# First pair's keys hashed in two halves, and the last output block transposed on TensorE

## Chip, cores and metric

The kernel runs on 1 core of one Trainium2 chip. The metric is device time in microseconds (us) for one execution: the median of three runs. The kernel before takes 908.99 us (runs: 909.02, 906.41 and 908.99). A separate profiled execution took 907.58 us, of which the profile's span is 905.8 us; all positions in time below are counted from the start of that span.

TensorE, the matrix engine, is PE in the profile, and its weight loads are PEld; VectorE is DVE, ScalarE is ACT, GpSimd is POOL and SyncE is SP. A "q" after an engine's name (SPq, ACTq) is its instruction queue, where it issues DMAs.

## What is computed

There are two parts. First an attention in which a query sees only the keys of its own hash bucket; the bucket is made of the signs of six random projections. Its output, turned into a matrix of 3072 tokens by 512, then goes through a feed-forward layer with a squared ReLU.

```python
# q, k, v: (4 batches, 8 heads, 768 positions, 64), proj: (64, 6)
q_bits = (einsum('bhsd,dk->bhsk', q, proj) > 0)
k_bits = (einsum('bhsd,dk->bhsk', k, proj) > 0)
mask   = bucket(q_bits)[..., :, None] == bucket(k_bits)[..., None, :]
scores = where(mask, q @ k.T / 8, -1e9)
attn   = softmax(scores)
x      = (attn @ v) arranged as (3072, 512)
h      = x @ w_in                    # (3072, 2048)
out    = (max(h, 0) ** 2) @ w_out    # (3072, 512)
```

## The kernel before: the parts that are touched

The attention works on 16 pairs of heads, one head on partitions 0 to 63 and the other on 64 to 127. For each pair it needs transposed queries and keys (`feat`) and their hash bits as numbers (`bits`): a score is the product of the bits of key and query, which is hugely negative if any bit differs, plus the product of their features. For all pairs but the first, `features` and `prepare` make these beside the scores of the pair before. The first pair has nothing to hide behind, so this is the head of the kernel.

```python
with tc.manual_schedule():              # every engine works in program order
    load_first()                        # q, k of pair 0: head 0 on SP's queue, head 1 on ACT's
    nc.vector.memset(busy, 1.0)
    keep_busy(8)                        # matmuls on dummy data
    make_identity(nc, ident)
    constants()                         # loads proj, see below
    load_pair(1); load_values(0)
    for i in range(2): load_weight(i)
    first_features(0, 0)                # 3 TensorE transposes of q, copied out by ACT
    first_features(0, 1)
    keep_busy(2, 256)
    first_features(1, 0)                # 3 TensorE transposes of k (keys 0 to 383), copied by DVE
    hash_bits(0, turn("hash"), (0,))    # projections of q: 4 matmuls, PSUM
    first_features(1, 1)                # keys 384 to 767
    banks = turn("hash")
    for c in range(2):
        hash_bits(0, banks, (1,), (c,)) # projections of k: 2 matmuls for each half
    keep_busy(4)
    signs(0, 0)                         # 4 ACT activations: the bits of q
    first_keys()                        # DVE: the bits of k
    for pr in range(NP):
        ...
        score(pr, 0)                    # keys 0 to 127
        score(pr, 1)
        ...                             # score(pr, 2) to (pr, 5); keys 384 on from (pr, 3)

def constants():
    nc.gpsimd.memset(projs, 0.0)
    for h in range(2):
        nc.gpsimd.dma_start(out=projs[h * D:(h + 1) * D, 0:N], in_=proj)
    ...

def first_keys():
    bits[0, 1] = t = all_bits[0][1]
    for c in range(2):                  # c: half of the keys
        ...
        for h in range(2):
            nc.vector.tensor_scalar(out=t[...], in0=hashed[0, 1][...], scalar1=0.0, op0=ALU.is_gt)
        nc.vector.tensor_scalar(out=t[:, cut], in0=t[:, cut], scalar1=spans, scalar2=bases, ...)

def turn(name):                         # a PSUM tile of two banks; 3 take turns
    return ps_s.tile([P, 2, 512], FP32, name=name, tag="turn")
```

The feed-forward layer multiplies by a scheme of Strassen's kind in two levels. One `product` makes seven small products; in the last one of the kernel, `use(m, ...)` is `fourth(m, ...)`, which adds up a block of 128 output columns by 256 tokens and closes it. The output comes out transposed (columns on partitions). `put_out` turns it in blocks of 32 by 32 on DVE and writes it with four DMAs, whose runs in DRAM are 32 values long.

```python
def product(n, w, at, bt, c11, c12, c21, c22, hook=None):
    ...
    c11(acc[1], one)                    # fourth(0)
    add(0, at(4), ...); two = keep(0, "two")
    add(2, at(3), ...); five = keep(2, "five")
    add(0, at(5), ...); three = keep(0, "three")
    add(2, at(6), ..., last=True)
    c12(acc[2], two)                    # fourth(1): closes columns 0 to 127, both halves
    c22(three, five)                    # fourth(3)
    add(0, at(2), bt["t4"], last=True)  # the last 8 matmul passes of the kernel
    c21(acc[0])                         # fourth(2): the last block

def fourth(n, one, two):
    add_to(out_block(1, 0, n), block(W, n), whole(one, two))
    close(1, 0, n)

def close(ih, jh, n):                   # columns 128 to 255 of the last block: each half by itself
    ...
    if (i, ih, jh, n // 2) == (NCHUNK - 1, 1, 0, 1):
        lo = n % 2 * QN
        put_out(i, ih, jh, n // 2, o[0][:, lo:lo + QN], lo)
    elif o[1] == 2:
        put_out(i, ih, jh, n // 2, o[0])

def put_out(i, ih, jh, n, o, lo=0):
    ot = p_y.tile([P, HN], FP32, name="ot", bufs=2)[:, 0:w]      # two buffers in turn
    nc.vector.transpose(out=ot, in_=o)
    for a in range(P // 32):
        queue = nc.gpsimd if (ih, jh) == (1, 1) else nc.sync
        if (i, ih, jh) == (NCHUNK - 1, 1, 0) and a % 2:
            queue = nc.scalar
        queue.dma_start(out=out[at, ...].rearrange("(c i) j -> i c j", i=32), in_=ot[...])
```

After that every engine reads a flag (`slow`) and jumps over a general version of the kernel, which these inputs don't need. SP waits for all outstanding DMAs, and the program ends.

Of the kernel before, what the change touches and what calls it, by code (L numbers as in the profile page):

```python
# [34 lines left out]
def kernel(  # L35
# [10 lines left out]
    nc = tc.nc  # L46
# [174 lines left out]
    def constants():  # L221
        N = NBITS
        nc.gpsimd.memset(projs, 0.0)
        for h in range(2):
            nc.gpsimd.dma_start(out=projs[h * D:(h + 1) * D, 0:N], in_=proj)
# [126 lines left out]
    def first_keys():  # L352

        bits[0, 1] = t = all_bits[0][1]
        for c in range(2):
            at = slice((2 + c) * NR_B, (3 + c) * NR_B)
            cut = slice(c * HS, (c + 1) * HS)
            for h in range(2):
                nc.vector.tensor_scalar(
                    out=t[h * D:h * D + NR_B, cut], in0=hashed[0, 1][at, h, 0:HS],  # L360
                    scalar1=0.0, scalar2=None, op0=ALU.is_gt,
                )
            nc.vector.tensor_scalar(
                out=t[:, cut], in0=t[:, cut], scalar1=spans, scalar2=bases, op0=ALU.mult,
                op1=ALU.add,
            )

# [188 lines left out]
    with tc.manual_schedule():  # L556
        load_first()
        nc.vector.memset(busy, 1.0)
# [11 lines left out]
        hash_bits(0, turn("hash"), (0,))  # L570
        first_features(1, 1)
        banks = turn("hash")
        for c in range(2):
            hash_bits(0, banks, (1,), (c,))
        keep_busy(4)
        signs(0, 0)
        first_keys()
# [3 lines left out]
        for pr in range(NP):  # L581
# [20 lines left out]
            score(pr, 0)  # L602
            score(pr, 1)
# [221 lines left out]
        def put_out(i, ih, jh, n, o, lo=0):  # L825


            w = o.shape[1]
            ot = p_y.tile([P, HN], FP32, name="ot", bufs=2)[:, 0:w]
            nc.vector.transpose(out=ot, in_=o)  # L830
            m0 = ih * HD + n * P
            at = slice(i * NCH + jh * HN + lo, i * NCH + jh * HN + lo + w)
            for a in range(P // 32):
                queue = nc.gpsimd if (ih, jh) == (1, 1) else nc.sync
                if (i, ih, jh) == (NCHUNK - 1, 1, 0) and a % 2:
                    queue = nc.scalar
# [3 lines left out]
                )  # L840

        def project(i):
# [12 lines left out]
            def close(ih, jh, n):  # L855
                o = outs[ih, jh, n // 2]
                o[1] += 1
                if (i, ih, jh, n // 2) == (NCHUNK - 1, 1, 0, 1):

                    lo = n % 2 * QN  # L860
                    put_out(i, ih, jh, n // 2, o[0][:, lo:lo + QN], lo)
                elif o[1] == 2:
                    put_out(i, ih, jh, n // 2, o[0])
# [357 lines left out]
```

## Time and profile before

| Engine | Busy, us | Share of the span | Instructions |
|---|---|---|---|
| PE | 884.4 | 98% | 4372 |
| PEld | 504.5 | 56% | 4372 |
| DVE | 697.6 | 77% | 1012 |
| ACT | 363.4 | 40% | 593 |
| POOL | 91.4 | 10% | 149 |

The granted TensorE clock is 0.996 of full speed over the span. The chain that ended last spends 93% of its time on PE and 3% on DMA. Read the page for the middle of the kernel, where PE is always busy; for its two ends, the totals hide everything, and the timeline and the chain have to be asked for the first 20 us and the last 20 us alone.

### The profile page before, as it was taken

The page shows a single profiled execution, that of the slowest core. Times are in us where ns is not written, and L with a number is a line of the kernel's source. Part 1 is how long each engine was busy: PE and PEld are TensorE (multiplying, and loading weights), DVE is VectorE, ACT ScalarE, POOL GpSimd, SP SyncE. Part 2 cuts the span into 40 slices and gives each one's busy share as a digit, 9 for nine tenths or more (in the row PEclk, how much of TensorE's full clock was granted, in tenths as well). Part 3 has the DMA queues.
Part 4 walks back from the last instruction along what each step waited for, and adds up shares of the span by engine and source line. Part 5 has one row for each costly group of instructions (what it writes and reads, how often), then busy time and mean ns, then how long its engine had stood idle before and what let it go on. Part 6 is the DMA issues. An engine that isn't in the chain of part 4 may idle for free.

```text
span 905.8 us, 11897 instructions
## 1 busy us (share of the span) xinstructions
PE 884.4 (98%) x4372; PEld 504.5 (56%) x4372; DVE 697.6 (77%) x1012; ACT 363.4 (40%) x593; POOL 91.4 (10%) x149
## 2 busy tenths in 40 slices
PE   8999999999999999999999999999999999999994
PEld 3444444444444444443688854445888644458884
DVE  5788899798998885887777776677778666777874
ACT  5878878887788761222211112221111122221110
POOL 2000000000000000564000011112000211100002
PEclk9999999999999999999999999999999999999998
DMA  9577769778977326999765735557757455545575
GB/s 180 107 146 139 198 175 204 172 251 210 233 182 162 112 99 185 279 273 287 253 219 159 178 67 151 152 151 221 278 150 183 75 151 152 149 130 159 144 188 82
DMA packets 253407, 158.14 MB, mean 175 GB/s; under 512 B 166496, under 2 KB 215648, under 8 KB 253344
## 3 DMA queue, kind: packets, MB, share of 16 engines
q1 hardware_dynamic: 218448, 84.04, 39.4%
q10 hardware_dynamic: 24160, 37.89, 14.4%
q0 software_dynamic: 10736, 35.40, 12.8%
q8 instruction: 36, 0.59, 0.3%
q14 instruction: 27, 0.22, 0.1%
HBM read 119.28 MB, written 38.01 MB: 174 GB/s over the span
## 4 chain that ended last, share of the span: by engine, by line
PE 93%; DMA 3%; DVE 2%; ACT 1%; issue 1%; ACTq 0%; DVEq 0%
PE acc L675 57%; PE st L385 17%; PE xo L412 14%; PE tot L430 3%; PE hash L337 2%; DMA w_unit<-w_in 2%; DMA k_nat<-in_k_dram 1%; ACT bits L347 1%; ACT e L389 0%; DVE peaks L716 0%; DVE b L765 0%; DMA out_dram<-ot 0%; DMA leaf<-w_out 0%; DVE h L764 0%; DVE t L491 0%
## 5 line engine op out<-in xcount | busy, mean ns | idle before, releaser
L389 ACT ACTIVATE e<-st 128x1024 f32<-128x1024 f32 x192 | 145.2, 810 | 67.7 <-PE st L385 62.7
L675 PE MATMUL acc<-x,w_unit 128*128 128x512 f32 x384 | 169.6, 593 | 1.8 <-DMA w_unit<-w_in 1.8
L385 PE MATMUL st<-feat,feat 64*128 64x512 f32 (+1 forms) x768 | 150.4, 483 | 0.0
L412 PE MATMUL xo<-e,v_nat 128*64 128x512 f32 (+1 forms) x768 | 134.8, 492 | 0.0
L675 PE MATMUL acc<-b,leaf 128*128 128x256 f32 x600 | 133.0, 379 | 0.0
L675 PE MATMUL acc<-t_x,w_unit 128*128 128x512 f32 x288 | 127.8, 593 | 0.0
L675 PEld LDWEIGHTS acc<-x,w_unit 128*128 128x128 f32 x384 | 72.8, 190 | 92.7 <-issue 89.2
L675 PEld LDWEIGHTS acc<-b,leaf 128*128 128x128 f32 x600 | 113.8, 190 | 17.1 <-issue 1.7
L412 PEld LDWEIGHTS xo<-e,v_nat 128*64 128x64 f32 x768 | 51.4, 136 | 82.4 <-issue 70.3
L675 PEld LDWEIGHTS acc<-t_x,w_unit 128*128 128x128 f32 x288 | 54.5, 190 | 69.8 <-issue 67.7
L385 PEld LDWEIGHTS st<-feat,feat 64*128 64x128 f32 x768 | 66.1, 188 | 34.9 <-issue 26.8
L402 DVE TENSOR_TENSOR total<-total,e 128x1536 f32<-128x1536 f32 x48 | 84.2, 1753 | 1.7
L764 DVE TENSOR_TENSOR h<-acc,two 128x512 f32<-128x512 f32 x24 | 16.6, 691 | 86.2 <-PE acc L675 86.2
L675 PE MATMUL acc<-t,leaf 128*128 128x256 f32 x336 | 76.6, 380 | 0.8 <-ACT one L682 0.4
L682 ACT COPY two<-acc 128x512 f32<-128x512 f32 (+1 forms) x45 | 21.9, 486 | 131.8 <-PE acc L675 113.3
L347 ACT ACTIVATE bits<-hash,lifts 32x384 bf16<-32x384 f32 x124 | 70.9, 572 | 7.1 <-issue 3.5
L675 PEld LDWEIGHTS acc<-t,leaf 128*128 128x128 f32 x336 | 63.6, 190 | 10.5 <-DVE t L491 1.1
L682 ACT COPY one<-acc 128x512 f32<-128x512 f32 (+1 forms) x45 | 21.9, 486 | 117.0 <-PE acc L675 75.2
L765 DVE SCALAR_TENSOR_TENSOR b<-h 128x512 f32<-128x512 f32 x96 | 64.2, 690 | 2.5
L385 PE MATMUL st<-bits,bits 64*128 64x256 bf16 (+1 forms) x384 | 63.2, 325 | 2.4 <-ACT e L389 1.2
L675 PE MATMUL acc<-b_t,leaf 128*128 128x256 f32 x240 | 54.2, 380 | 1.3 <-issue 1.3
L675 PEld LDWEIGHTS acc<-b_t,leaf 128*128 128x128 f32 x240 | 45.4, 190 | 8.1 <-issue 2.0
(125 smaller groups left out, 871.4 us busy)
## 6 DMA issues: line engine op xcount, KB each, us to landing
leaf<-w_out ACTq DMA_DIRECT2D x142, 256.0 KB, 3.0
w_unit<-w_in SPq DMA_DIRECT2D x24, 896.0 KB, 6.0
raw<-in_moe_w_in_dram SPq DMA_DIRECT2D x16, 512.0 KB, 5.5
raw<-in_moe_w_out_dram SPq DMA_DIRECT2D x16, 512.0 KB, 4.7
w_out<-sums POOLq DMA_DIRECT2D x16, 448.0 KB, 7.0
v_nat<-in_v_dram SPq DMA_DIRECT2D x16, 384.0 KB, 4.9
x_all<-x_t SPq DMA_DIRECT2D x16, 384.0 KB, 3.1
x<-x_all POOLq DMA_DIRECT2D x3, 2048.0 KB, 13.0
```

The source lines that it names most:

```text
L337: nc.tensor.matmul(out=banks[g * NR_B:(g + 1) * NR_B, h, 0:HS], lhsT=projs[rows], rhs=feat[pr, w][rows, c * HS:(c + 1) * HS], start=True, ...
L347: nc.scalar.activation(out=t[h * D:h * D + NR_B, c * HS:(c + 1) * HS], in_=hashed[pr, w][at, h, 0:HS], func=ACTF.Sign, scale=HUGE, bias=li ...
L385: nc.tensor.matmul(out=st[:, h, 0:hi - lo], lhsT=src[pr, 1][rows, key], rhs=src[pr, 0][rows, lo:hi], start=first, stop=not first,)
L389: nc.scalar.activation(out=e[:, :, lo:hi], in_=st[:, :, 0:hi - lo], func=ACTF.Exp, scale=scale)
L402: nc.vector.tensor_tensor(out=totals[pr], in0=in0, in1=weights[pr, kt][:, :, 0:S], op=ALU.add)
L412: nc.tensor.matmul(out=xo[h * D:(h + 1) * D, lo:hi], lhsT=nat[pr, "v_nat"][:, h, kt * D:(kt + 1) * D], rhs=weights[pr, kt][:, h, lo:hi], s ...
L430: nc.tensor.matmul(out=tot[g * 32:(g + 1) * 32, 0:HS], lhsT=ones, rhs=src[:, h, c * HS:(c + 1) * HS], start=src is totals[pr], stop=src is ...
L675: nc.tensor.matmul(out=acc[to], lhsT=a(i), rhs=b(i), start=first and i == 0, stop=last and i == n - 1, skip_group_check=True,)
L682: nc.scalar.copy(out=t, in_=acc[of])
L764: nc.vector.tensor_tensor(out=h, in0=one, in1=two, op=ALU.add)
L765: nc.vector.scalar_tensor_tensor(out=out[:, r], in0=h, scalar=0.0, in1=h, op0=ALU.max, op1=ALU.mult)
```

## The change

At the head of the kernel it makes two changes. The projections (`proj`) are loaded from ACT's queue, behind the keys, instead of from GpSimd's. The keys of the first pair are hashed and weighed in two halves: keys 0 to 383 at once, before the second half of the keys is even transposed, and keys 384 to 767 only after the first score tile, since the scores need them only from `score(0, 3)` on. The purpose is to let the first scores start earlier.

At the end, the last 128 output columns of the last block (two halves of 256 tokens) are no longer turned in 32 by 32 blocks on DVE. Two TensorE transposes each turn them whole into PSUM, ACT copies one half out and DVE the other, and each half is written with one DMA, whose runs in DRAM are 128 values long. Of the four DMAs of the block before, the two that went over ACT's queue go over GpSimd's. The purpose is to shorten the chain behind the last matmul.

```diff
     def constants():
-        nc.gpsimd.memset(projs, 0.0)
-        for h in range(2):
-            nc.gpsimd.dma_start(out=projs[h * D:(h + 1) * D, 0:N], in_=proj)
...
-    def first_keys():
-        bits[0, 1] = t = all_bits[0][1]
-        for c in range(2):
...
+    def first_keys(c, banks):
+        if c == 0:
+            bits[0, 1] = all_bits[0][1]
+        t = bits[0, 1]
+        hash_bits(0, banks, (1,), (c,))
+        at = slice((2 + c) * NR_B, (3 + c) * NR_B)
+        cut = slice(c * HS, (c + 1) * HS)
+        for h in range(2):
             nc.vector.tensor_scalar(
+                out=t[h * D:h * D + NR_B, cut], in0=banks[at, h, 0:HS],
+                scalar1=0.0, scalar2=None, op0=ALU.is_gt,
             )
+        nc.vector.tensor_scalar(
+            out=t[:, cut], in0=t[:, cut], scalar1=spans, scalar2=bases, op0=ALU.mult, op1=ALU.add,
+        )
...
     with tc.manual_schedule():
+        nc.vector.memset(busy, 1.0)
+        nc.vector.memset(projs, 0.0)
         load_first()
-        nc.vector.memset(busy, 1.0)
+        for h in range(2):
+            nc.scalar.dma_start(out=projs[h * D:(h + 1) * D, 0:NBITS], in_=proj)
...
         hash_bits(0, turn("hash"), (0,))
+        signs(0, 0)
+        first_keys(0, turn("hash"))
         first_features(1, 1)
-        banks = turn("hash")
-        for c in range(2):
-            hash_bits(0, banks, (1,), (c,))
         keep_busy(4)
-        signs(0, 0)
-        first_keys()
...
             score(pr, 0)
+            if pr == 0:
+                first_keys(1, turn("hash"))
             score(pr, 1)
...
                 if (i, ih, jh) == (NCHUNK - 1, 1, 0) and a % 2:
-                    queue = nc.scalar
+                    queue = nc.gpsimd
...
+        def put_last(n, o):
+            row, col = n // 2, n % 2
+            tp = ps_m.tile([P, 512], FP32, name=f"acc{col}")[:, 0:QN]
+            for t in range(QN // P):
+                nc.tensor.transpose(out=tp[:, t * P:(t + 1) * P], in_=o[...], identity=ident)
+            ot = p_y.tile([P, HN], FP32, name="ot", bufs=2)[:, 0:QN]
+            if col:
+                nc.scalar.copy(out=ot, in_=tp)
+            else:
+                nc.vector.tensor_copy(out=ot, in_=tp)
+            lo = (NCHUNK - 1) * NCH + col * QN
+            (nc.sync if col else nc.scalar).dma_start(
+                out=out[lo:lo + QN, HD + row * P:HD + (row + 1) * P].rearrange(
+                    "(t p) j -> p t j", p=P),
+                in_=ot.rearrange("p (t j) -> p t j", j=P),
+            )
...
                 if (i, ih, jh, n // 2) == (NCHUNK - 1, 1, 0, 1):
-                    lo = n % 2 * QN
-                    put_out(i, ih, jh, n // 2, o[0][:, lo:lo + QN], lo)
+                    put_last(n, o[0][:, n % 2 * QN:(n % 2 + 1) * QN])
```

## The prediction

> **What bounds the kernel now.** I read the page first: PE is busy 98% of 905.8 us, so only what lengthens or shortens PE's own line counts, and PE's line has slack only at its two ends. The change touches nothing between. So I asked the chain of waits for the first 20 us.
>
> ```profile
> 1.28 5.19 DMA k_nat<-in_k_dram
> ...
> 6.51 0.55 PE tp L300 x3
> 7.06 1.35 PE hash L337 x8
> 8.41 0.48 PE tp L300 x3
> 8.89 1.49 PE hash L337 x8
> 10.37 0.97 PE xo L317 x4
> 11.34 0.80 issue
> 12.14 6.12 PE st L385 x42
> ```
>
> The columns are start, length, what. Until 6.5 us the first keys are on their way. Then everything is one line: transpose keys, hash queries, transpose the other keys, hash both halves, dummy matmuls, and at 12.14 us the first score. Two views say what holds these steps: the waits of the first 32 us (first line below), and VectorE's timeline.
>
> ```profile
> PEld hash L337 <- DMA projs<-in_proj_dram: 0.4, 1, 0.4
> ```
>
> ```profile
> 10.50 1.12 DVE L359 TENSOR_SCALAR bits<-hash 32x384 bf16<-32x384 f32 x2 [1.02 <-PE hash L337]
> 11.66 0.38 DVE L363 TENSOR_SCALAR bits<-bits,spans,bases 128x384 bf16<-128x384 bf16 x1
> 12.07 1.13 DVE L359 TENSOR_SCALAR bits<-hash 32x384 bf16<-32x384 f32 x2
> ```
>
> The projections come 0.4 us late. And DVE begins the bits of keys 0 to 383 only at 10.50, when both halves are hashed; they are done at 12.04, and the scores start. So the first score waits for DVE, and DVE waits for a hash of keys that no one needs yet.
>
> For the other end, DVE's timeline from 892 us on:
>
> ```profile
> 893.48 0.71 DVE L830 STREAM_TRANSPOSE ot<-o 128x512 f32<-128x512 f32 x1
> 894.12 0.38 DVE L815 TENSOR_TENSOR tmp<-three,five 128x256 f32<-128x256 f32 x1
> 894.54 0.43 DVE L815 TENSOR_TENSOR o<-sum,tmp 128x256 f32<-128x256 f32 x1
> 896.03 0.45 DVE L830 STREAM_TRANSPOSE ot<-o 128x256 f32<-128x256 f32 x1 [1.07 <-DMA out_dram<-ot]
> 896.40 0.38 DVE L815 TENSOR_TENSOR o<-sum,acc 128x256 f32<-128x256 f32 x1
> 897.64 0.45 DVE L830 STREAM_TRANSPOSE ot<-o 128x256 f32<-128x256 f32 x1 [0.85 <-DMA out_dram<-ot]
> ```
>
> PE's last matmul ends at 894.19. DVE then waits twice for a free `ot` buffer, and its last transpose ends at 898.09, with nothing computed in between that takes long. The issues behind it are worse (SyncE's queue, the timeline cut at 896 us; ScalarE's shows the same at 896.92):
>
> ```profile
> 896.86 2.23 SPq L837 DMA_DIRECT2D out_dram<-ot  x1
> ```
>
> The others of its kind take 0.3 to 0.6 us. The last two DMAs of either queue go out at 899.19 and 899.65 and land by 902.03. Meanwhile SP jumps over the general version; the waits of its queue have `SPq L1051 <- SPq L1051: 2.7`, from 900.86 to 903.57. Then some twenty semaphore checks and the last barrier take 2.2 us to 905.8.
>
> **What the Trainium skill says.** "VectorE: DVE Perf Modes", section "The three transpose paths": DVE transposes in 32 by 32 blocks, TensorE turns a full 128 by 128 but into PSUM, which a copy must empty. The trace agrees on the cost: three fp32 transposes take 0.55 us, 384 columns out of PSUM 0.48 us on ACT and 0.56 us on DVE. "DMA: Bandwidth & Descriptors", section "Anatomy of one DMA — SWDGE (gpsimd) path": a fixed cost of about 2 us, nearly all of it completion. Here output DMAs at the end take 2.1 to 4.3 us to landing, median 2.8, so fewer DMAs behind each other save issues, not that floor. "Runtime: NRT & Kernel Launch", section "Instruction fetch mechanics": engines stream instructions in 16 KiB blocks, and a jump out of the window waits for a fetch. SP's 2.7 us at its jump fits; ACT's took only 0.4 us, so it is not certain to recur. I take the 2.2 us stall for such a fetch too: a 16384-byte packet of the instruction queue starts at 896.9 and takes 1.8 us. That is a guess.
>
> **Head, step by step.** (a) The projections' 64 small packets go behind the keys on ACT's queue. The last packet of those keys starts at about 5.6 us and the keys land at 6.47, so I put the projections at 6.6 to 6.9 instead of 7.52. The queries' hash (from 6.99) then runs through: from 7.57 its six remaining passes took 0.84 us, and all eight together, on separate parts of the array, should take the same, so it ends at 7.83, not 8.41. (b) The keys' first half, two matmuls: the same two took 0.83 us (8.82 to 9.65). They end near 8.6. (c) DVE: 1.12 + 0.38 us and gaps, as before 1.54 us from its start to its end: from 8.7 to 10.25. (d) ACT's four activations for the queries' bits: 2.35 us, now from 7.95, done at 10.3. Both inputs are there by 10.3, and the dummy matmuls (transposes 8.6 to 9.1, then 1.0 us) are through at 10.1. First score at 10.35: 1.8 us earlier. (e) The second half's hash now stands between two score tiles; two fp32 matmuls of 384 columns with two passes each keep PE 0.7 us (second half's start less the first's, 9.54 - 8.82). Net: 1.8 - 0.7 = 1.1 us. ACT doesn't take it back: its exponentials are about 1.6 us for a key tile, like PE's 1.62. The second half's bits, on DVE, come at about 14.5, and `score(0, 3)` needs them after 15.9.
>
> All that follows moves 1.1 us forward as one piece: pair 1's loads land at about 13, DVE takes them at 18.27; the first weights land at about 17 to 18, DVE needs them at 20.02.
>
> **End, step by step,** on the old clock. c22 comes before the last eight matmuls in program order, so PE's two transposes for that block now stand before them, and they wait for DVE's sum, ready at 894.97. PE, which would have gone on at 892.5, stands still until 895.05. Then 2 transposes 0.4 us, with the eight passes (0.217 us apart) overlapping: last matmul out at 897.2, 3 us later than before. DVE's sum 0.4 us: 897.65. Transposes 0.45: 898.15. DVE's copy of 256 columns, 0.4: 898.6. One DMA on ACT's queue, 0.45 to issue and 2.3 from its start to landing: 901.0. The `ot` buffer is free in time: GpSimd issues its two DMAs (0.65 us each) by 895.5, landed by about 898.1. The ACT half goes out at about 896.5. The old clock had 902.03 for the last landing and 903.57 for SP past its jump; SP now issues its last DMA near 896.9 instead of 900.20 and has jumped by 900.3 at the latest. So the closing checks start at 901.0 instead of 903.57, and I expect a saving of 2.6, of which I keep 2.2 for stragglers. Sum: 1.1 + 2.2 = 3.3 us.
>
> **The rivals.** First: the new wait of PE takes everything back. PE idles 2.5 us behind DVE; if transposes or semaphores cost 0.3 us more at each of four hand-overs, or if GpSimd's final drain (6.1 us before, from 892.27 to 898.37) runs 6.1 us from 895.6, to 901.7, or ACT's jump takes SP's 2.7 us (to 902.4), the end is worth only 1 to 1.5 us; total about 906. For it speaks that all three closing paths lie within 1.5 us of each other. Second: ACT's two extra issues, 0.5 us each, delay its table load (1.28 us, from 1.98) to about 3, ending at 4.3; its first copy is at 5.53, so this is hidden. But if the projections' packets queue until 7.5, (a) is void and the head gives 0.6 us: total 906. Third: a slot of the three PSUM tiles is lost to the second hash, and `score(0, 2)` waits for DVE's compare behind it; the head then gives 0.5 us. Against it: the compare ends 1.2 us after the hash, and PE works over 1.6 us on `score(0, 1)` meanwhile. Fourth: the saving is eaten in the middle. PE waits once there, 1.8 us for `w_unit<-w_in` at 419 us, a DMA of 13.7 us; its issue is set by PE's own progress, so it should move along, but its length can change by a microsecond either way.
>
> **Range and chances.** The three runs before spread over 2.6 us, the profiled one is 907.58, and the mean of all four is 908.0; a median of three is uncertain by about 1 us. 908.3, between that and the median, less 3.3 is 905.0. Adding spread of the runs, the rivals' 1 to 2 us and a possible fetch stall or its absence (2 us), eight in ten lie in 902.4 to 907.8. 2% is 18 us; the head lasts 12 us and the end 12, so neither can reach it: same 0.98.
>
> **What would show it.** Right: the first score near 10.4 us, no wait for `projs`, `hash` matmuls after the first score tile, PE idle about 2.5 us near the end in front of its transposes, last landing about 2 us after DVE's last copy. Wrong: a `projs` wait at the first hash, the first score later than 11.2, PE waiting for ACT at the third score tile, a closing chain through GpSimd's drain or through ACT's jump, or a changed wait in the middle.

## The result and the profile after

The changed kernel takes 906.82 us (median of six runs, 905.91 to 909.7) and the kernel before, on the same chip, 908.04 us (six runs, 906.41 to 909.02). The ratio is 0.9994, with a 95% interval of 0.9975 to 1.0013: no difference that can be measured; the interval leaves room for a saving of some 2.3 us at most. The prediction was 905.0 us, with eight chances in ten for 902.4 to 907.8. The total is inside. The saving of 3.3 us that it was worked out from is not.

The two profiled spans are 905.8 us before and 904.1 us after, so the profile seems to show 1.7 us of the 3.3. To see where they lie I cut every span into three pieces at two points of the trace that all kernels here share: the start of the second pair's scores, which closes the head, and the start of VectorE's sum `o` for columns 0 to 127 of the last block, where the code of the end begins.

| Span, us | Head | Middle | End | All |
|---|---|---|---|---|
| before | 31.69 | 861.33 | 12.78 | 905.8 |
| after | 31.76 | 859.58 | 12.74 | 904.1 |

Neither end got shorter. The 1.7 us lie in the middle, which the change doesn't touch. So each end has to be asked what it gained and what it gave back.

**Head.** The chain that ended last in the first 20 us of after; columns are start, length and what:

```profile
1.99 5.64 DMA projs<-in_proj_dram
...
7.76 1.18 PE hash L334 x12
8.95 0.56 ACT bits L344
...
10.71 0.58 ACT bits L344
11.34 1.77 PE st L384 x11
13.11 0.77 PE hash L334 x4
13.88 4.44 PE st L384 x30
```

Before, this chain ran through the keys and TensorE. Now it begins with the projections, which are on their way for 5.64 us and land at 7.63 (and 7.94 for the second). The first hash starts at 7.76, not at 6.99. Then ScalarE's four activations, the queries' bits, take up to 11.29, and the scores wait for them. The first score tile of one head starts at 10.74, the other's at 11.34; before it was 12.14 us. At 13.11 the moved hash takes 0.77 us out of the row of scores. VectorE, which the prediction had ready at the same time as ScalarE, was done with the first half's bits at 10.58:

```profile
9.05 1.12 DVE L358 TENSOR_SCALAR bits<-hash 32x384 bf16<-32x384 f32 x2 [1.02 <-PE hash L334]
10.20 0.38 DVE L362 TENSOR_SCALAR bits<-bits,spans,bases 128x384 bf16<-128x384 bf16 x1
```

**End.** TensorE's timeline of after from 889 us on; the bracket holds the idle time ahead of a group and what ended it:

```profile
889.75 1.03 PE L676 MATMUL acc<-b_t,leaf 128*128 128x256 f32 x4
893.33 0.62 PE L847 MATMUL acc<-ident,o 128*128 128x128 f32 x2 [2.56 <-DVE o L816]
893.75 3.43 PE L676 MATMUL acc<-b_t,leaf 128*128 128x256 f32 x8
897.69 0.44 PE L847 MATMUL acc<-ident,o 128*128 128x128 f32 x2 [0.52 <-DVE o L816]
```

TensorE stands still for 2.56 us in front of the transposes, as predicted. But the eight passes behind them then take 3.43 us, 0.427 us apart, where the prediction had 0.217. The table of stretches says why (the columns: stretch, its length, busy time of PE, PEld, DVE, ACT and POOL with their instructions, granted TensorE clock, DMA share, GB/s):

```profile
894.00:896.00 2.00, 2.00 (x6) 1.55 (x6) 0.00 (x0) 0.36 (x1) 0.10 (x1) 0.50 0.78 138
```

The clock has fallen to half, from 893.45 to 896.86. VectorE's last two operations, and the first waits of SP's queue in that stretch:

```profile
897.22 0.42 DVE L816 TENSOR_TENSOR o<-sum,acc 128x256 f32<-128x256 f32 x1 [3.94 <-PE acc L676]
898.17 0.42 DVE L854 COPY ot<-acc 128x256 f32<-128x256 f32 x1 [0.53 <-PE acc L847]
```

```profile
SPq L1070 <- SPq L1070: 6.5, 2, 3.5
```

The last copy ends at 898.6 and its DMA goes out at 898.62. The 6.5 us of SP are two things that the line doesn't keep apart. From 895.46 to 898.40 it is its jump over the general version. The other 3.5 us, by the semaphore records, are a wait for one DMA, the last: 15 of its 16 parts have landed by 900.47, the sixteenth lands at 902.15, SP goes on at 902.17, and the rest of its closing list takes the 1.9 us to the end.

### The profile page after: what moved, and what is told of

Read it like the earlier page. It is cut to its first block, busy times and chain, and to the rows that moved or that the text cites. A ratio compares the mean times of both kernels' runs of the same rounds, so it can differ in the third digit from the quotient of the medians.

```text
span 904.1 us, 11898 instructions
## 1 busy us (share of the span) xinstructions
PE 886.7 (98%) x4376; PEld 506.3 (56%) x4376; DVE 697.6 (77%) x1012; ACT 364.2 (40%) x594; POOL 91.7 (10%) x148
## 4 chain that ended last, share of the span: by engine, by line
PE 91%; DMA 4%; DVE 2%; ACT 1%; issue 1%; POOL 0%; ACTq 0%; DVEq 0%
PE acc L676 55%; PE st L384 17%; PE xo L411 14%; DMA w_unit<-w_in 3%; PE tot L429 3%; PE hash L334 2%; ACT bits L344 1%; DMA projs<-in_proj_dram 1%; DVE peaks L717 0%; DMA out_dram<-ot 0%; DVE b L766 0%; ACT e L388 0%; DVE ot L830 0%; DVE h L765 0%; DVE o L816 0%
## 6 DMA issues: line engine op xcount, KB each, us to landing
x<-x_all POOLq DMA_DIRECT2D x3, 2048.0 KB, 13.1
```

## The experiments

All were cut at the same two points. "First score" is where a score matmul first starts; "last out" is the end of the last pass of the kernel's products, counted from the start of the end piece; "landing" is when the last part of the last output DMA has landed, counted likewise. "Time" is the run's own measured time, single except where said.

| Run | First score | Head | Middle | Last out | Landing | End | Time |
|---|---|---|---|---|---|---|---|
| before | 12.14 | 31.69 | 861.33 | +1.16 | +9.01 | 12.78 | 908.04 (median) |
| before_again | 12.20 | 31.76 | 860.63 | +1.16 | +8.95 | 12.53 | 906.69 |
| h_only | 10.94 | 31.95 | 861.09 | +1.16 | +9.08 | 11.89 | 906.71 |
| t_only | 12.37 | 31.93 | 861.26 | +5.62 | +10.61 | 12.68 | 907.71 |
| after | 10.74 | 31.76 | 859.58 | +5.84 | +10.81 | 12.74 | 906.82 (median) |
| h_early | 10.83 | 31.60 | 861.08 | +5.42 | +10.31 | 12.38 | 906.83 |
| t_warm | 10.91 | 31.93 | 864.19 | +4.16 | +9.15 | 11.08 | 909.01 |
| t_defer | 10.78 | 31.81 | 861.93 | +1.16 | +10.62 | 12.55 | 908.05 |
| t_defer_own | 11.06 | 32.08 | 860.36 | +1.16 | +7.31 | 10.20 | 904.41 |
| h_noins | 13.23 | 32.80 | 861.57 | +4.16 | +8.38 | 10.31 | 906.44 |
| h_noins2 | 10.74 | 30.87 | 860.27 | +5.03 | +9.44 | 11.36 | 904.27 |
| h_sp | 11.22 | 32.23 | 860.49 | +4.16 | +8.83 | 10.76 | 905.26 |
| t_best | 10.81 | 31.82 | 860.71 | +1.16 | +7.66 | 10.52 | 904.82 |
| best | 10.86 | 30.99 | 861.34 | +1.16 | +7.67 | 9.45 | 903.75 (median) |

The kernel before, measured beside the single runs, gave single times between 906.9 and 911.6 us, and the middle alone differs by 2.3 us (859.58 to 861.93) among kernels that share its code (t_warm aside). So single times decide nothing here; the pieces do.

### The change taken apart: before_again, h_only, t_only

My theory was that the head gains at its first score and gives it back, that the end loses what it gains to the clock, and that the middle is scatter. The rival was that the middle's 1.7 us is an effect of the earlier head. `before_again` is the kernel before without an edit, `h_only` is after with before's end, `t_only` is after with before's head.

```diff
 # h_only, against after
-                    queue = nc.gpsimd
+                    queue = nc.scalar
-                    put_last(n, o[0][:, n % 2 * QN:(n % 2 + 1) * QN])
+                    lo = n % 2 * QN
+                    put_out(i, ih, jh, n // 2, o[0][:, lo:lo + QN], lo)
 # t_only, against after (before's load of proj on GpSimd and before's order again)
-        signs(0, 0)
-        first_keys(0, turn("hash"))
         first_features(1, 1)
+        banks = turn("hash")
+        for c in range(2):
+            hash_bits(0, banks, (1,), (c,))
         keep_busy(4)
+        signs(0, 0)
+        first_keys()
```

> The kernel before, once more, for the scatter of its three stretches: head (start of pair 1's scores, 31.76 us in the chain of the first profile), middle (from there to the start of VectorE's sum o for columns 0 to 127 of the last block, 893.02) and tail (from there to the end of the span, 12.78). Theory 'middle is scatter': head within 0.2 us, tail within 0.5 us, middle off by up to 2 us, mostly at the wait for w_unit at 419 us. Rival 'the change moved the middle': middle within 0.3 us of the first profile, 1.7 us longer than after's.

> The changed head alone, with the end of before. Theory 'late projections and an inserted hash': pair 1's scores start at 31.8, as in after (31.83) and before (31.76); the first hash waits for projs until about 7.6 again, and the second hash takes 0.7 to 0.8 us between the first two key tiles. Rival 'the head lost its gain by chance in that one profile': they start at 30.7. Tail as before: 12.8 us.

> The changed end alone, with the head of before. Theory 'clock and stragglers': PE stands still some 2 us in front of its transposes, its clock drops, the last eight passes are 0.43 us apart instead of 0.22, and the tail is 12.8 us as in before and after; if the clock's drop happens to fall after the passes, it is 11 to 11.5. Rival 'the tail's changes need the changed head': none expected. Head 31.76.

Measured: the head piece is 31.69 and 31.76 us in the two profiles of before, 31.93 in `t_only` (before's head), and 31.76 and 31.95 in after and `h_only` (the new head). The new head has its first score 1.2 to 1.4 us earlier than the first profile of before, and arrives at the second pair at the same time or later. The middle is 860.63 in `before_again`, 0.7 shorter than in the other profile of the same kernel, and 861.09 in `h_only`. So the rival does not hold: with the new head alone, the middle is no shorter than in `before_again`. `t_only` has the end of after, 12.68 us, with the head of before: what happens at the end belongs to the end. Its clock fell too, from 894.78 to 898.20.

`h_only` also shows that before's end is not always 12.78: here it is 11.89. The long DMA issue on SP, which the prediction counted in, is not in it.

What the middle's scatter is made of can be seen at one place. The waits of TensorE from 415 to 470 us, first in before and then in after (us in total, times, longest):

```profile
PE acc L675 <- DMA w_unit<-w_in: 1.8, 1, 1.8
```

```profile
PE acc L676 <- DMA w_unit<-w_in: 1.1, 1, 1.1
```

The weights that TensorE waits for there were 13.73 us on their way before and 13.02 us after. That is 0.7 of the 1.7 us. Laid side by side instruction by instruction, TensorE's records show after gaining at four more places, 0.5 us at 222 us and 0.2 each at 461, 532 and 649. `before_again`, which has no edit, gains 0.4 at the first of them and 0.2 at the last. No run shows that the change had a hand in any of them.

### The head: who holds the first score

After `h_only` there were two questions. Do the projections come late because they stand behind the keys on ScalarE's queue, or because nothing small gets through while the first loads run? And does the moved hash cost what the earlier start gains? `h_early` issues the projections ahead of everything, on GpSimd's queue; `h_sp` ahead of the queries, on SP's.

```diff
 # h_early, against after (memset of projs moved to GpSimd as well)
-        load_first()
         for h in range(2):
-            nc.scalar.dma_start(out=projs[h * D:(h + 1) * D, 0:NBITS], in_=proj)
+            nc.gpsimd.dma_start(out=projs[h * D:(h + 1) * D, 0:NBITS], in_=proj)
+        load_first()
 # h_sp: the same with nc.sync; the memset stays on VectorE
```

> After, but the projections are the first thing on GpSimd's queue, ahead of everything else. Theory 'late projections': they land before 6 us, the first hash starts when the keys are transposed and its copy is out (7.1 to 7.4), ACT's bits of the queries are done by 10.7 instead of 11.29, and pair 1's scores start 0.5 to 0.7 us earlier than in after, at 31.2. Rival 'ACT's or DVE's chain bounds the head, not the projections': no change, 31.8.

> After, with the projections first on SP's queue, ahead of the queries and keys of head 0, where no other transfer stands before them. Theory 'the projections come late because they share the DMA engines with the first loads': they land before 5 us and the first hash starts when the features are there, at 7.1 to 7.4; the keys of head 0 come up to 1 us later, so pair 1's scores start between 31.2 and 31.8. Rival 'small packets are slow wherever they are queued': the first hash still waits for them until 7.6.

The DMAs of the first microseconds; `h_early` first, then `h_sp` (KB each, ns of one issue, first and last issue):

```profile
L559 POOL DMA_DIRECT2D projs<-in_proj_dram x2: 543/618/692, 1.3 to 2.0; - x2
DMA to landing us min/median/max: 5.7/5.7/5.7
```

```profile
L559 SPq DMA_DIRECT2D projs<-in_proj_dram x2: 575/580/586, 0.9 to 1.6; - x2
DMA to landing us min/median/max: 3.0/3.1/3.3
```

On GpSimd's queue the projections went out 0.7 us earlier than in after and took 5.7 us; the hash's wait for them fell only to 0.2 us. On SP's queue, ahead of the queries, they took 3.0 to 3.3 us and the wait was gone. But the queries behind them went out at 2.21 us instead of 0.77 and landed at 6.08 instead of 3.93, and all that hangs on them came later:

```profile
6.21 0.85 PE L297 MATMUL tp<-ident,q_nat 128*128 128x128 f32 x6 [1.10 <-DMA q_nat<-in_q_dram]
8.46 0.87 PE L334 MATMUL hash<-feat,projs 64*32 64x384 f32 x12 [0.70 <-issue]
```

The queries' transposes start at 6.21 instead of 4.87, the hash at 8.46 instead of 7.76, and the second pair 0.5 us later than in after. So it is not the place behind the keys in ScalarE's queue that makes the projections late; they were as slow first in GpSimd's, and where they were put ahead of the queries, the queries paid. That the loads take the DMA engines from each other is my reading of this, not shown by itself.

Nor did `h_early` bring the projections early. By the semaphore records its second load of them landed at 7.78 instead of 7.94 us, 0.16 earlier, and ScalarE's bits (8.78 instead of 8.94), the later score tile (11.18 instead of 11.34) and the second pair follow by the same 0.16. In 13 of the 14 profiles ScalarE's bits start 1.0 us after that second landing (in before 8.52 after 7.52); only in `h_sp`, where it is at 4.86, do the late queries hold them. So in after the second load of the projections sets when the later score tile starts.

`h_noins` and `h_noins2` hash both halves of the keys before the scores, so nothing is inserted. `h_noins` puts both hashes into one PSUM tile that otherwise only the dummy matmuls use, `h_noins2` into two tiles in turn:

```diff
 # h_noins, against after
+        first_features(1, 1)
         ...
-        first_keys(0, turn("hash"))
-        first_features(1, 1)
+        banks = void.rearrange("p (h n) -> p h n", h=2)
+        first_keys(0, banks)
+        first_keys(1, banks)
 ...
-            if pr == 0:
-                first_keys(1, turn("hash"))
 # h_noins2, against after (and the same last two lines out)
+        first_features(1, 1)
         hash_bits(0, turn("hash"), (0,))
         signs(0, 0)
         first_keys(0, turn("hash"))
-        first_features(1, 1)
+        first_keys(1, turn("hash"))
```

> After, with the second half of the keys transposed before the first hash (while PE waits for the projections anyway) and hashed right behind the first half, so that nothing stands between the first two key tiles. The hashes of the keys go to an otherwise idle PSUM tile. Theory 'the inserted hash gives back 0.8 us': first scores at 10.8 to 11.3, pair 1's scores at 31.0 instead of 31.76. Rival 'later work (ACT) takes up the shift': pair 1's scores still at 31.6 to 31.9.

> As h_noins, but the two hashes of the keys go to two PSUM tiles in turn, since in h_noins the second hash and the dummy matmuls, in the same tile, waited for VectorE's compares of the first (1.35 and 1.24 us on PE). Theory 'the inserted hash gives back 0.8 us': first scores at 10.7 to 11.4, both halves of the keys hashed before 9.3, pair 1's scores at 30.8 to 31.2 instead of 31.8. Rival 'later work (ACT) takes up the shift': 31.6 to 31.9.

`h_noins` missed: its first score came at 13.23 us, for a reason of my own making. TensorE's timeline:

```profile
10.20 0.83 PE L334 MATMUL xo<-feat,projs 64*32 64x384 f32 x4 [1.35 <-DVE bits L358]
12.28 1.02 PE L314 MATMUL xo<-busy 128*64 128x512 bf16 x4 [1.24 <-DVE bits L358]
```

The second hash and the dummy matmuls write into the tile that VectorE is still comparing, so TensorE waits for it twice, 2.6 us in all. It says nothing about the insertion. `h_noins2` has no such wait:

```profile
7.77 1.45 PE L334 MATMUL hash<-feat,projs 64*32 64x384 f32 x16 [0.17 <-DMA projs<-in_proj_dram]
10.74 0.37 PE L384 MATMUL st<-bits,bits 64*128 64x512 bf16 x1 [0.55 <-ACT bits L344]
11.34 0.37 PE L384 MATMUL st<-bits,bits 64*128 64x512 bf16 x1 [0.22 <-ACT bits L344]
```

All hashes are one group of 1.45 us, and the scores start at 10.74 and 11.34, exactly as in after, since ScalarE's bits hold them in both. With nothing inserted at 13.1 us, the second pair starts at 30.87: 0.9 earlier than in after, 0.8 earlier than before. So the insertion had eaten the whole gain of the head, and it was not needed, because TensorE had idle time ahead of the scores to put that hash into.

### The end: the clock

In `t_warm` TensorE doesn't stand still ahead of the transposes. Eleven dummy matmuls fill the gap (each is recorded as two passes); the transposes start no later for them, 1.99 us after the start of the end piece as in after.

```diff
 # t_warm, against after, at the top of put_last
+            if col:
+                idle = ps_t.tile([P, 512], FP32, name="tp")
+                for _ in range(11):
+                    nc.tensor.matmul(
+                        out=idle[:, 0:P], lhsT=ident, rhs=ident, start=True, stop=True)
```

> After, with 11 dummy fp32 matmuls of 128 columns on PE in front of the third block's transposes, where PE stands still for some 2.5 us; nothing waits for their result. Theory 'the standstill lowers PE's clock': the clock stays at full speed, the last eight passes are 0.217 us apart instead of 0.43, the last matmul ends 4.2 us after the reference (the start of VectorE's sum for columns 0 to 127) instead of 5.4 to 5.8, and the tail from that reference to the end is 11.0 to 11.4 instead of 12.4 to 12.7. Rival 'the passes are slow for another reason (weights behind transposes, DMA)': spacing stays 0.43 and the tail 12.7.

TensorE's timeline, and the stretch:

```profile
895.39 2.62 PE L848 MATMUL tp<-ident 128*128 128x128 f32 x22
898.11 0.44 PE L853 MATMUL acc<-ident,o 128*128 128x128 f32 x2
898.38 1.89 PE L676 MATMUL acc<-b_t,leaf 128*128 128x256 f32 x8
```

```profile
898.00:900.00 2.00, 1.89 (x11) 1.61 (x10) 0.05 (x1) 0.37 (x1) 0.87 (x2) 1.00 0.80 121
```

The clock stays at full speed, the eight passes take 1.89 us instead of 3.43, the last one is out at +4.16 instead of +5.84, and the end is 11.08 us: 1.66 us shorter, all of it from the clock. The run as a whole took 909.01 us, since its clock was at half for 3.41 us from 223.46 on as well, far from the edit. There, too, TensorE had stood still before (its timeline):

```profile
222.47 2.11 PE L334 MATMUL hash<-feat,projs 64*32 64x384 f32 x16 [2.16 <-DVE feat L321]
```

Does a standstill always do this? `h_noins`, `h_noins2`, `h_sp` and `h_early` have after's end too, each with the same gap of 2.55 or 2.56 us, and their last passes are out anywhere between +4.16 and +5.42. The clock's own records give the reason. In every run the clock changes only after a whole number of stretches of 3.413 us, counted from its first rise (887.47 us is 260 of them), and that first rise comes at another moment in each run, 4.2 to 7.3 us. So the gap falls differently into these stretches:

```
           gap of TensorE    stretch          of the gap in it   clock after the stretch
after      890.77 to 893.33  890.03 to 893.45  2.56 us           0.5 from 893.45
h_early    892.11 to 894.66  891.99 to 895.40  2.55              0.5 from 895.40
h_noins2   890.58 to 893.14  890.87 to 894.28  2.27              0.5 from 894.28
t_only     892.62 to 895.18  891.37 to 894.78  2.16              0.5 from 894.78
h_sp       892.16 to 894.72  889.82 to 893.23  1.07              1.0
                             893.23 to 896.65  1.49              1.0
h_noins    893.80 to 896.36  891.80 to 895.22  1.42              1.0
                             895.22 to 898.63  1.14              1.0
```

A stretch with 2.16 us of the gap or more was followed by half clock, one with 1.49 or less was not. Where the gap was cut in two by the border of a stretch, nothing happened, and the end is 10.3 to 10.8 us long. All 14 profiles, from end to end, bear this out. They have 3660 stretches that began at full clock; of these the 18 in which TensorE stood idle for 2.00 us or more in all were followed by half clock, and none of the 3642 others was, with up to 1.83 us idle (in before, 892.60 to 896.01, behind the last pass). The 2.16 us of `t_warm` at 222 us, in the stretch from 220.05 to 223.46, are one of the 18.

So whether the change loses its gain at the end is drawn anew in each execution. As an estimate from these numbers: with a gap of 2.56 us at a random place and a limit somewhere between 1.83 and 2.00, the clock falls in some 60 to 70% of the executions. It fell in four of the six runs of the table.

The Trainium skill has this in "TensorE: Matmul & The Clock Gate", section "Part 1: The HAM clock gate": TensorE is held at half clock after an idle window of about 3.4 us, and the windows run freely, whatever the kernel does. The records here agree: 3.413 us, with a start that differs from run to run. But the window need not be idle throughout: 2.00 of its 3.41 us were enough.

### The end: the transposes moved behind the last passes

The gap itself can be avoided. `t_defer` issues the last eight passes first and the third block's transposes behind them. `t_defer_own` also gives the last two blocks output buffers of their own, not shared with the block before.

```diff
 # t_defer, against after; last is true for the kernel's last product
-            c22(three, five)
-            add(0, at(2), bt["t4"], False, True)
+            if last:
+                add(0, at(2), bt["t4"], False, True)
+                c22(three, five)
+            else:
+                c22(three, five)
+                add(0, at(2), bt["t4"], False, True)
 # t_defer_own: that, and in put_last
-            ot = p_y.tile([P, HN], FP32, name="ot", bufs=2)[:, 0:QN]
+            ot = p_y.tile([P, QN], FP32, name="tmp", bufs=2)
```

> After, with the third block's sum and transposes put behind the last eight matmul passes instead of in front. Theory 'PE's standstill and its jump set the end': last matmul ends 1.2 us after the reference as in before, PE's last transpose near 3.0, its jump over the general version (4.1 us in three profiles) ends near 7.2, and the tail is 8.8 to 9.3. Rival 'the last DMA's landing sets the end': the last copy still waits for the ot buffer until 5.0 (two DMAs of GpSimd), its DMA lands at 7.5 to 9.2, and the tail is 9.1 to 10.8.

> As the deferred one, and the last two blocks are copied into other buffers (those of the sums, of 256 columns), so that the last copy doesn't wait for an earlier DMA. Theory 'PE's jump sets the end': the last DMA lands near 5.5 to 6 but PE's jump still ends near 7.2, tail 8.8 to 9.0, at most 0.3 us shorter than with the shared buffer. Rival 'landing sets the end': the tail falls by another 1.5 us, to 7.3 to 7.8.

`t_defer` missed: the last pass is out 4.7 us earlier (+1.16), and the end is 12.55. VectorE's timeline:

```profile
895.60 0.41 DVE L820 TENSOR_TENSOR o<-sum,acc 128x256 f32<-128x256 f32 x1
900.92 0.42 DVE L858 COPY ot<-acc 128x256 f32<-128x256 f32 x1 [4.92 <-DMA out_dram<-ot]
```

The last copy stands for 4.92 us in front of the `ot` buffer, which still feeds the output DMAs that the change moved to GpSimd's queue (15 of the 16 parts of the last of them were there by 898.82, the sixteenth at 900.85). The wait that the change was to remove from the end is back, longer than the 0.85 us of before. With own buffers it is gone; VectorE's copy in `t_defer_own`, and the wait of SP:

```profile
895.24 0.42 DVE L858 COPY tmp<-acc 128x256 f32<-128x256 f32 x1 [0.53 <-PE acc L851]
```

```profile
SPq L1075 <- SPq L1075: 4.0, 1, 4.0
```

The copy starts 4.4 us sooner than in `t_defer`, counted from the common point, and the last DMA lands at +7.31. The end is 10.20 us, 2.5 shorter than in after, but 1.2 to 1.4 longer than I expected: SP's own jump, from 896.37 to 900.38, now ends after the last landing (899.75). GpSimd's final drain was no better: by the records it ended at 901.81, SP's closing list at 901.80.

`t_best` was to free SP early: its last DMAs go over ScalarE's and GpSimd's queues.

```diff
 # t_best, against t_defer_own
-                if (i, ih, jh) == (NCHUNK - 1, 1, 0) and a % 2:
-                    queue = nc.gpsimd
+                if (i, ih, jh) == (NCHUNK - 1, 1, 0):
+                    queue = (nc.scalar, nc.gpsimd)[a % 2]
 ...
-            (nc.sync if col else nc.scalar).dma_start(
+            nc.scalar.dma_start(
```

> As t_defer_own, with SP's queue free of the last block: its DMAs go over ACT's and GpSimd's queues, so that SP can jump early. In t_defer_own SP passed its jump only at 900.38, 7.9 us after the reference, later than PE (7.2). Theory 'the jumps of SP and PE set the end': SP is past it by 6 us after the reference, PE at 7.2, tail 8.7 to 9.2 instead of 10.2. Rival 'the landing of the last DMA sets the end'[...]: landing at 7.5 to 8, tail 9.3 to 10.

Neither theory held. SP was past its jump at 893.21 and through its list at 901.29, but GpSimd's final drain, which starts once its last DMA is issued, took 6.93 us from 895.28, to 902.22, and set the end at 10.52.

### What the end waits for: the last landing, and what delays it

My expectations for `t_defer`, `t_defer_own` and `t_best` spoke of TensorE's jump. In before TensorE's queue has issued its last work at 892.3 (the last pass ends at 894.19), and its jump over the general version, 3.9 us, is over at 896.2, unseen. The end of before is set by SP's jump: it is over at 903.57, 1.5 us after the last landing (in `before_again` 1.3, in `h_only` 0.6). In after TensorE can only jump behind the last transposes, at 898.29, and comes out at 902.43. In the first runs that fitted: the end came 1.6 to 1.9 us after it. But the landing of the last output DMA fits better. These come from the records of the trace, since no view has a line for them:

```
              PE jump       last landing        end, us after
              ends   15 of 16   16th    span    jump   16th part
after        902.43   900.47   902.15  904.08   1.65   1.93
t_only       904.01   902.15   903.80  905.87   1.86   2.07
h_early      903.28   901.54   902.98  905.05   1.77   2.07
t_warm       905.51   904.01   905.27  907.19   1.68   1.92
h_noins      902.97   901.91   902.75  904.67   1.70   1.92
h_noins2     900.82   899.97   900.58  902.50   1.68   1.92
h_sp         901.87   900.26   901.56  903.48   1.61   1.92
t_defer      901.17   903.47   904.36  906.28   5.11   1.92
best         899.94   898.58   900.01  901.79   1.85   1.78
```

`t_defer` tells them apart: there the jump is over 3.2 us before the last landing, and the end follows the landing. In after, too, SP waited for the landing until 902.17 and asked for TensorE's flag only at 903.07, when it had been there for over half a microsecond. So the end of after is set by the sixteenth part of one DMA.

Why is that part late? The last DMA of after has 272 packets, 16 times 17. The records have 255 of them between 899.5 and 900.2 and the other 17 from 900.9 to 901.7. In between, from 899.99 to 900.96, lies a 16384-byte packet of an instruction queue that carries 36 such packets in the whole run, and the last before it was at 866.8. It is the same in `t_only`, `h_early`, `t_warm` and `h_sp`: the last 17 packets start within 0.1 us of the end of that packet (902.62, 901.75, 903.67, 900.35). In `h_noins` and `h_noins2` it ends at 901.56 and 899.39, while other parts are still under way, and the 17 can't be told apart. The packet begins 1.0 to 1.7 us after TensorE's jump in each of them, and in before 1.47 us after it (893.76, jump at 892.29), well ahead of the last DMAs. So I take it for the fetch of TensorE's jump target; the trace doesn't name the engine, and I ran no kernel without the jump. The Trainium skill, in "DMA: Bandwidth & Descriptors", section "Queues, rings and completion order", says that a DMA is split over up to 16 rings, and that each DMA engine finishes a whole packet before it turns to another queue. The 17 packets that follow one of 16384 bytes agree, if what the trace lists as packets may be taken for the page's, which no run here shows. By this reading the part is late because the change brings TensorE's jump and the last DMA together: in after they are 0.33 us apart, in before the jump came 7.4 us ahead of the last issue. `best` is not free of it either (898.58 and 900.01). The gain from a part in time would be less than the 1.7 us by which it is late. TensorE's own jump is over only at 902.43, and in after the end comes 1.0 us after SP has gone past TensorE's flag (set at 902.54); as an estimate from these numbers, the end would be near 903.5 instead of 904.08.

### The best of both: best

`best` takes the head of `h_noins2` and the end of `t_defer_own`; its other last DMAs go over SP's and ScalarE's queues and none over GpSimd's.

```diff
 # best, against after: the edits of h_noins2 and t_defer_own, and
-                    queue = nc.gpsimd
+                    queue = nc.scalar
 ...
-            (nc.sync if col else nc.scalar).dma_start(
+            nc.scalar.dma_start(
```

> Both ends mended: the keys' two hashes right behind each other before the first scores (h_noins2), the third block's transposes behind the last passes, the last two blocks in their own buffers (t_defer_own), and no DMA of the last 128-column pair on GpSimd's queue, whose final drain (6.9 us) ended t_best. Theory 'ends add up': pair 1's scores at 30.9, GpSimd's drain ends before PE's jump, and the tail from the reference is 9.2 to 9.8; against before that is 0.9 at the head and 2.9 to 3.4 at the end, so 904 us against 908, ratio 0.9955 to 0.9965. Rival 'the middle's scatter hides it': ratio 0.998 to 1.000 with an interval that holds 1.

Its head is 30.99 us, its end 9.45: 0.7 and 3.3 us less than before (2.4 less than the shortest end with before's code, 11.89), with the middle at 861.34, the same as in before. The times agree: 903.75 us (median of five, 903.56 to 905.02) against 908.1 us (nine, 905.97 to 909.89), a ratio of 0.9955, with a 95% interval of 0.994 to 0.997. That is less than 2%, but it is clearly below 1, and its interval lies below that of after. TensorE's last work in it, and ScalarE's:

```profile
894.33 0.77 PE L850 MATMUL acc<-ident,o 128*128 128x128 f32 x4 [0.83 <-DVE o L819]
```

```profile
895.21 0.93 ACTq L859 DMA_DIRECT2D out_dram<-tmp  x2
```

The four transposes stand together behind all products, VectorE's copy follows at 895.14 (898.17 in after), and the last issue is over at 896.14. GpSimd's drain (896.9), SP's jump (898.75), TensorE's jump (899.94) and the last landing (900.01) are all through within the time in which the DMAs land.

## Why the prediction was right and where it was wrong

That the time is inside the range is luck: 3.3 us were predicted, the two ends together gave nothing in the profiles, and the measured 1.2 us between the medians is within the scatter, as the ratio says. What held was the bound: the change can reach the head and the end alone, and neither is a per cent of the time.

**Head, step (a), failed.** The projections were put at 6.6 to 6.9 us. They landed at 7.63 and 7.94, later than before (6.78 and 7.52), although they were issued behind the keys on a queue with nothing else in it. This was the second rival, and it came true in full. `h_early` and `h_sp` show that the place in one queue was the wrong thing to look at: beside or behind the first large loads the small one took 5.1 to 5.9 us on GpSimd's and on ScalarE's queue alike, in all runs; only ahead of the queries on SP's queue did it take 3.0 to 3.3.

**Steps (b) and (c), the keys' half and VectorE,** were right in size: about 8.9 us instead of 8.6 for the hash, 10.58 instead of 10.25 for the bits, both late mainly through (a).

**Step (d) was right in itself and carried (a)'s error on.** ScalarE's 2.35 us were right to the hundredth, but they start 1.0 us after the second load of the projections has landed, at 8.94 instead of 7.95: done at 11.29 instead of 10.3. So ScalarE alone holds the scores, and the two heads' tiles start at 10.74 and 11.34 instead of both at 10.35. The gain is 0.8 us from the later tile's start, not 1.8.

**Step (e) was right:** 0.7 predicted, 0.77 in the chain, and 0.9 by `h_noins2`. (The difference it was read from, 9.54 less 8.82, ends with TensorE's wait for VectorE's copy of the keys, so the agreement is in part luck.) With it the head is 0.8 less 0.8, nothing. The mechanism of the head was right, its first term was not.

**Third rival:** no PSUM slot was lost. **Fourth rival:** the middle did change, by 1.7 us in the profile, to the good; the two profiles of before differ by 0.7 there.

**End.** The standstill of TensorE was predicted (2.55 us) and measured (2.56), and at full clock the rest would have held, as `t_warm` shows: last pass at +4.16 against a predicted +4.18 (897.2 on the old clock). The step that failed is the sum from the standstill to the last landing, with two terms that were not in it. From the start of the end piece the prediction has the landing at +7.98 and, with 2.2 us of closing, the end at 10.18. Measured are +10.81 and 12.74. The difference of 2.56 is 1.66 for the clock (`t_warm`), about 1.1 for the sixteenth part of the last DMA (3.53 us from issue to landing instead of 2.4; its other parts needed 1.85), less 0.3 in a closing list that is shorter than I had put it. Before's end of 12.78 was also a long one: 11.89 and 12.53 in the other two profiles. The first rival had the new wait of TensorE take everything back, and in the total it did, but not by its hand-overs, which were as long as I took them, nor by GpSimd's drain (over at 899.08) or ScalarE's jump (0.4 us). It did so through what the standstill does to the clock, which `t_warm` shows, and through the late part of the last DMA, whose cause is argued and not shown. TensorE's own jump, 4.14 us behind its last transposes, was on none of the prediction's closing paths: in `t_warm`, at full clock, it is over at +9.39, and with the 1.1 us that after needs from there to the end (902.54 for the flag, 1.0 behind it), an estimate, the predicted end at 10.18 was out of reach by 0.3 us even with the landing in time.

The guess that SP's long issue of 2.23 us in before was such a fetch stays open. In `before_again` SP and ScalarE have it again (2.13 and 2.07 us, from 896.29 and 896.35), and again a 16384-byte packet starts within 0.05 us of it (896.34). `h_only` has the packet (897.60) and no long issue, but there SP's issue ends as the packet starts, and ScalarE's 0.07 us later.

## What to carry to other kernels

Before an operation is put on an engine ahead of work that it could do at once, ask where that engine's program order makes it stand still: a wait of 2.56 us cost 1.7 us more through the clock, and the same transposes behind the last passes, with buffers of their own and a free queue, took 2.4 to 3.3 us off the end, depending on the profile of before's end that it is compared with. Moving work out of a wait and into a row of work that is the bound gains nothing: look first for idle time of the bound engine ahead of the row, as for the hash here. And when two ends of a span are changed, cut both spans at common points before reading any total, since the untouched middle moved by more than either end.

## What was not expected of the hardware

- The TensorE clock changed only at the borders of stretches of 3.413 us that begin anew in each execution. It fell to 0.50 after each stretch with 2.00 us or more of standstill, and stayed after all those with 1.83 or less, so that the same gap cost 1.7 us in one run and nothing in another.
- TensorE's jump over the general version took 3.3 to 4.5 us and SP's 2.6 to 4.0, ScalarE's and VectorE's 0.4 to 0.5.
- One of the 16 parts of a small DMA landed 0.6 to 1.7 us after the others, in nine kernels, and in five of them its packets could be seen to begin as a 16384-byte instruction packet ended.
- The projections' two loads, 64 small packets together, took 5.1 to 5.9 us each beside the first large loads, and 3.0 to 3.3 us ahead of the queries on SP's queue. ScalarE's work on the queries' hash started 1.0 us after the second of them landed, in 13 of 14 profiles.
- GpSimd's final drain took 5.0 to 6.9 us from its last DMA, and in two kernels it was still running when the last DMA had landed.
